# Moving one batch's k and q flips into the next pass, W1 loads ahead of k, q and v, and split work later in the first pass of a fused attention + MLP kernel

## The chip, the cores and the metric

One core of one Trainium2 chip. The metric is the device time of a run in microseconds (us). A change counts as faster or slower when it moves the time by over 2%. Differences under 1% matter here, so the experiments were timed in five rounds beside runs of the kernel before on the same chip (three rounds for two of them), and compared by ratio. All runs were in the fast state, with a granted TensorE clock of 0.991 to 1.0.

## The reference

```python
attn = softmax(q @ k.T / 8)                   # 8 batches, 16 q heads on 4 kv heads, 384 tokens, dim 64
x    = (attn @ v) as [8, 384, 1024]
u    = x + lam * (w_tok @ (alpha1 * x + beta1))     # token mixing, w_tok is 384 x 384
out  = u + lam * (relu((alpha2 * u + beta2) @ w_ch1) @ w_ch2)   # 1024 -> 4096 -> 1024
```

All inputs and the output are float32; the kernel multiplies in bfloat16. W1 is w_ch1 and W2 is w_ch2.

## The kernel before: the parts that matter

The kernel makes eight passes, one for each batch's MLP. A pass has a first half, h (16 chunks, each of which reads one W1 tile of 512 KB from a ring of five; the ReLU of its result is hT), and a second half, ch, which multiplies hT by W2 (W2 stays in SBUF). The attention of batch b+1 is woven into pass b. Its q and k must first be turned ("flipped") so that the head dimension lies on partitions. For batch 1 TensorE does this inside the first pass's h; from batch 2 on it is done by DMA transposes that SP issues. The last flips of a pass, those of a2 (alpha2 * u) into a2T, feed the next pass's h. In the first pass VectorE also does the "split", which writes the rows of alpha2 and lam as sums of bfloat16 parts, and a "spread" copies such rows to all partitions with matmuls. PE, the matmul engine TensorE, writes its sums into banks of PSUM; the kernel uses a bank again only when VectorE or ScalarE has read it.

```python
def flip_k(b):   # one DMA transpose of 12 blocks of 128 x 128
    nc.sync.dma_start_transpose(out=kT..., in_=k2s[b]...)
def flip_q(b, i=0, n=NP):   # two head pairs a call: 6 blocks; four calls for a batch
    nc.sync.dma_start_transpose(out=qT[:, i:i + n]..., in_=qrs[b]...)

def main(b):            # one pass; every yield lets woven work be emitted
    for c in range(NCH):                  # h: 16 chunks, two slots per h group
        ...  # 2 x 8 matmuls with the chunk's W1 tile; ReLU on ScalarE or VectorE
        if b or c + RING < NCH:
            load_w1(b * NCH + c + RING)   # refills the ring, from GpSimd's queue
        if b == 0 and c == NCH - 1:
            load_next(2)                  # k casts, q and v loads of batch 2
            for i in range(RING):
                load_w1(NCH + i)
    ...                                   # ch: 6 groups of 32 matmuls, eight slots each

# slots of ch in which pass b emits the flips for batch b + 2 (load_k, load_next: not for b == 0)
((1, load_k), (2, load_next), (34, flip_k), (36, flip_q, 0, 2), (37, flip_q, 2, 2),
 (42, flip_q, 4, 2), (43, flip_q, 6, 2))[2 * (b == 0):]
```

A slot fixes only where an instruction stands in the order of its engine. When it runs is decided by the engine and by its waits.

The softmax here doesn't subtract the row's maximum and nothing guards it: scores larger than these inputs give would overflow.

## Time and profile before

| | before |
|---|---|
| time, median (lowest to highest of 4) | 805.95 us (805.39 to 806.19) |
| PE busy, span of the profiled run | 788.9 us of 805.1 |
| first h matmul of passes 1, 2, 3, 4 | 30.89, 135.39, 234.06, 330.71 us |
| second to third pass; third to fourth | 98.67; 96.65 us |
| DMA row of the page | transfer engines at nine tenths or more of each slice until about 200 us |

The distance from one pass's first h matmul to the next one's is the most useful number of this case. From the third pass on it is 96.64 or 96.65 us in nearly every kernel below; what is over that in "second to third" is lost in the second pass. The prediction further down shows the lines of the profile that carry the argument.

### The profile page before, as it was taken

What the parts mean: (1) busy time and instruction counts of PE and PEld (TensorE: products, weight loads), DVE (VectorE), ACT (ScalarE), POOL (GpSimd) and SP (SyncE); (2) the same over time, 40 slices, a digit from 0 to 9 for tenths busy, and PEclk for the clock granted to TensorE, in tenths of its full rate; (3) what the DMA queues carried; (4) which work ended last, traced back from release to release, by engine and by line L of the source; (5) the groups of instructions that cost most, each with busy time, mean ns of one, the idle gap of its engine ahead of it and who ended that gap; (6) DMA issues with size and microseconds to landing.
All of it is one profiled execution on the core that took longest, in us unless ns stands there. A gap on an engine that the chain in (4) does not pass through costs nothing.

```text
span 805.1 us, 14151 instructions
## 1 busy us (share of the span) xinstructions
PE 788.9 (98%) x6056; PEld 452.3 (56%) x6123; DVE 342.6 (43%) x669; ACT 226.5 (28%) x309; POOL 179.4 (22%) x234
## 2 busy tenths in 40 slices
PE   7999999999999999999999999999999999999997
PEld 4766555655556555565555655556555655556545
DVE  7652465224552165422662236622366224552122
ACT  6623431223312334123321233222431224312100
POOL 7235430333003410135002340023400330003000
PEclk9999999999999999999999999999999999999999
DMA  9999999999269972899439991399915995139611
GB/s 186 196 207 198 203 203 182 184 198 144 54 129 184 198 112 57 151 190 197 72 78 164 195 199 50 86 176 195 166 44 117 162 198 91 48 61 181 89 40 40
DMA packets 234991, 113.17 MB, mean 141 GB/s; under 512 B 84392, under 2 KB 228784, under 8 KB 234928
## 3 DMA queue, kind: packets, MB, share of 16 engines
q0 software_dynamic: 170768, 83.47, 78.9%
q1 hardware_dynamic: 63616, 28.40, 14.5%
q8 instruction: 48, 0.79, 0.4%
q10 hardware_dynamic: 544, 0.39, 0.2%
q14 instruction: 15, 0.12, 0.0%
HBM read 170.53 MB, written 12.58 MB: 227 GB/s over the span
## 4 chain that ended last, share of the span: by engine, by line
PE 96%; DVE 1%; DMA 1%; issue 1%; POOL 0%; ACT 0%; POOLq 0%
PE ch L439 41%; PE h L406 40%; PE sc L214 4%; PE sc L249 4%; PE sc L270 4%; DMA stage<-in_moe_w_tok_dram 1%; PE h L165 1%; PE tok L270 1%; PE av L249 0%; PE ut L287 0%; DMA a2T<-a 0%; POOL v L110 0%; DVE hT L416 0%; DVE hT L525 0%; PE tp L200 0%
## 5 line engine op out<-in xcount | busy, mean ns | idle before, releaser
L439 PE MATMUL ch<-w,hT 128*128 128x512 bf16 (+2 forms) x1533 | 346.1, 370 | 4.4 <-issue 1.1
L406 PE MATMUL h<-a2T,w 128*128 128x384 bf16 (+1 forms) x2016 | 331.6, 326 | 2.5 <-DMA a2T<-a 1.5
L406 PEld LDWEIGHTS <-w 128*128 128x128 bf16 x2016 | 196.6, 98 | 133.1 <-issue 2.1
L133 POOL DMA_DIRECT2D w<-in_moe_w_ch_dram x128 | 112.0, 877 | 535.1 <-PE h L406 521.4
L439 PEld LDWEIGHTS <-hT 128*128 128x128 bf16 x1600 | 144.6, 98 | 152.6 <-issue 10.0
L223 ACT ACTIVATE es<-sc 128x1024 bf16<-128x1024 f32 x126 | 121.4, 1023 | 187.7 <-PE sc L214 178.8
L416 DVE TENSOR_SCALAR hT<-h,bias 128x384 bf16<-128x384 f32 x128 | 79.1, 618 | 219.0 <-PE h L406 218.5
L414 ACT ACTIVATE hT<-h,bias 128x384 bf16<-128x384 f32 x128 | 74.3, 581 | 304.8 <-PE h L406 304.2
L444 DVE TENSOR_TENSOR o<-ch,vecs 128x512 f32<-128x512 f32 (+2 forms) x50 | 33.4, 669 | 108.6 <-PE ch L439 108.6
L249 PEld LDWEIGHTS <-es 128*128 128x128 bf16 x1008 | 38.3, 97 | 13.2
L270 PEld LDWEIGHTS <-wtokT 128*128 128x128 bf16 x576 | 37.3, 98 | 13.6 <-DVE a L264 1.7
L214 PE MATMUL sc<-qT,kT 64*128 64x384 bf16 (+2 forms) x576 | 41.9, 271 | 1.2
L249 PE MATMUL sc<-v,es 128*128 128x65 bf16 x1008 | 39.8, 193 | 0.0
L254 DVE RECIPROCAL rinv<-sc 128x6 f32<-128x6 f32 x56 | 10.8, 193 | 67.4 <-PE sc L249 66.4
L277 DVE TENSOR_TENSOR x<-sc,x 128x384 f32<-128x384 f32 x56 | 31.0, 553 | 20.0 <-PE sc L270 20.0
L270 PE MATMUL sc<-a,wtokT 128*128 128x128 bf16 x504 | 37.3, 219 | 0.4
L214 PEld LDWEIGHTS <-kT 64*128 64x128 bf16 x576 | 21.7, 94 | 23.8 <-issue 18.4
L445 DVE TENSOR_TENSOR o<-o,x 128x512 f32<-128x512 f32 (+2 forms) x50 | 33.5, 670 | 1.7
L262 DVE TENSOR_TENSOR a1f<-x,vecs 128x384 f32<-128x384 f32 x56 | 31.6, 564 | 1.9
L264 DVE TENSOR_TENSOR a<-a1f,vecs 128x384 bf16<-128x384 f32 x56 | 31.4, 561 | 1.9
L281 DVE TENSOR_TENSOR a<-x,vecs 128x384 bf16<-128x384 f32 x56 | 31.3, 558 | 1.9
L255 DVE TENSOR_TENSOR x<-sc,rinv 128x384 f32<-128x384 f32 x56 | 31.2, 558 | 1.9
(75 smaller groups left out, 204.8 us busy)
## 6 DMA issues: line engine op xcount, KB each, us to landing
w<-in_moe_w_ch_dram POOLq DMA_DIRECT2D x136, 512.0 KB, 8.9
out_dram<-o SPq DMA_DIRECT2D x47, 256.0 KB, 2.0
q_raw<-in_q_dram POOLq DMA_DIRECT2D x28, 192.0 KB, 8.5
kst<-in_k_dram SPq DMA_DIRECT2D x16, 192.0 KB, 3.1
w<-in_moe_w_ch_dram POOLq DMA_DIRECT2D x1, 2048.0 KB, 16.5
w<-in_moe_w_ch_dram POOLq DMA_DIRECT2D x8, 256.0 KB, 10.0
v<-in_v_dram POOLq DMA_DIRECT2D x24, 64.0 KB, 8.6
a2T<-a SPq DMA_TRANSPOSE x56, 2.3
```

The lines of the kernel that those rows point to most:

```text
L133: nc.gpsimd.dma_start(out=t, in_=w1src[:, :, c * CW * P:(c + 1) * CW * P])
L214: nc.tensor.matmul(out=sc[:, hh, k % 4:k % 4 + n], lhsT=kT[r, sk, 2 * p // G, :], rhs=qT[r, p, st:st + n, :], start=True, stop=True)
L223: nc.scalar.activation(out=e, in_=sc, func=EXP, scale=scale_qk)
L249: nc.tensor.matmul(out=av[:, hh, sq, :], lhsT=ess[k // 4][:, m % 2, k % 4, :], rhs=vb[:, sk, hk, :], start=(sk == 0), stop=(sk == NST - 1))
L262: nc.vector.tensor_tensor(out=t, in0=x[:, :, cols(p)], in1=bc(g1, p), op=MUL)
L270: nc.tensor.matmul(out=ps[:, tt, :], lhsT=wtokT[:, st, tt * P:(tt + 1) * P], rhs=a1s[p][:, st, :], start=(st == 0), stop=(st == NST - 1 an ...
L406: nc.tensor.matmul(out=ps[:, :n], lhsT=w1[:, dt, j * P:(j + 1) * P], rhs=a2T[:, dt, :n], start=(dt == 0), stop=(dt == NDT - 1))
L414: nc.scalar.activation(out=hT[:, nt, :], in_=ps[:, :S], func=RELU, bias=c1)
L416: nc.vector.tensor_scalar(out=hT[:, nt, :], in0=ps[:, :S], scalar1=c1, scalar2=0.0, op0=ADD, op1=mybir.AluOpType.max)
L439: nc.tensor.matmul(out=ps[:, lo:hi], lhsT=hT[:, nt, ms * P:(ms + 1) * P], rhs=w2[:, nt, dw * 512 + lo:dw * 512 + hi], start=(nt == 0), sto ...
L444: nc.vector.tensor_tensor(out=o[:, lo:hi], in0=ps[:, lo:hi], in1=lam_t[:, c], op=MUL)
L445: nc.vector.tensor_tensor(out=o[:, lo:hi], in0=o[:, lo:hi], in1=x[:, ms, c], op=ADD)
```

## The change

Its intent: take the flips of batch 2 out of the busy end of the first pass, where they delay the a2T flips that the second pass waits for, and put them "late" in the second pass's h; load the W1 tiles first; spread the split of VectorE so that it does not hold a PSUM bank.

```diff
-                turns = {1: [(split, 2, 4)], 4: [(k_transpose, 0)], 8: [(q_transpose, 0, 2, "av")], 12: [(k_transpose, 2)]}
+                turns = {4: [(split, 2, 4, 0)], 8: [(split, 2, 4, 1)], 12: [(k_transpose, 0)],
+                         16: [(q_transpose, 0, 2, "av")], 20: [(k_transpose, 2)]}
...              # the other q transposes: 16 + 4 * i -> 24 + 4 * i; the spreads: 29 -> 34 and 45 -> 50
             if b == 0 and c == NCH - 1:
-                load_next(2)
                 for i in range(RING):
                     load_w1(NCH + i)
+                load_next(2)
...
+            moves = []
+            if b == 1:       # slots of h in the second pass
+                moves = [(0, 46 + 4 * i, flip_q, 2, 2 * i - 2, 2) if i else (0, 46, flip_k, 2) for i in range(5)]
+            if 0 < b < B - 2:      # later passes: as before
+                moves += [(1, 1, load_k, b + 2), (1, 2, load_next, b + 2), (1, 34, flip_k, b + 2), ...]
```

More of the change, by code (lines that the diff above doesn't have):

```diff
@@ L350, in side @@
             if b == 1:
-                turns = {1: [(split, 2, 4)], 4: [(k_transpose, 0)], 8: [(q_transpose, 0, 2, "av")], 12: [(k_transpose, 2)]}
+                turns = {4: [(split, 2, 4, 0)], 8: [(split, 2, 4, 1)], 12: [(k_transpose, 0)],
+                         16: [(q_transpose, 0, 2, "av")], 20: [(k_transpose, 2)]}
                 for i in range(3):
-                    turns[16 + 4 * i] = [(q_transpose, 2 + 2 * i, 2, "av")]
+                    turns[24 + 4 * i] = [(q_transpose, 2 + 2 * i, 2, "av")]
                 for i in range(4):
-                    turns[29 + 4 * i] = [(spread, (2 * i, 2 * i + 1), (1, 3), "tp", "ACT")]
+                    turns[34 + 4 * i] = [(spread, (2 * i, 2 * i + 1), (1, 3), "tp", "ACT")]
                 for i in range(2):
-                    turns[45 + 4 * i] = [(spread, range(4 * i, 4 * i + 4), (3, 4), "av", "ACT")]
+                    turns[50 + 4 * i] = [(spread, range(4 * i, 4 * i + 4), (3, 4), "av", "ACT")]
             return turns, {
@@ L555 @@
             us = side(b + 1) if b + 1 < B else ({}, {})
-            if b + 2 < B:
-                for u, f, *a in ((1, load_k), (2, load_next), (34, flip_k), (36, flip_q, 0, 2), (37, flip_q, 2, 2),
-                                 (42, flip_q, 4, 2), (43, flip_q, 6, 2))[2 * (b == 0):]:
-                    us[1].setdefault(u, []).append((f, b + 2, *a))
+            moves = []
+            if b == 1:
+                moves = [(0, 46 + 4 * i, flip_q, 2, 2 * i - 2, 2) if i else (0, 46, flip_k, 2) for i in range(5)]
+            if 0 < b < B - 2:
+                moves += [(1, 1, load_k, b + 2), (1, 2, load_next, b + 2), (1, 34, flip_k, b + 2), (1, 36, flip_q, b + 2, 0, 2),
+                          (1, 37, flip_q, b + 2, 2, 2), (1, 42, flip_q, b + 2, 4, 2), (1, 43, flip_q, b + 2, 6, 2)]
+            for i, u, *m in moves:
+                us[i].setdefault(u, []).append(m)
             done = [0, 0]
```

## The prediction

> **What bounds the kernel now.** I read the page first, for the busy shares and the slices; then the chain of waits around the ends of the passes; then the list of PE's waits; then the timelines of SP and PE where the chain left PE; last the DMA view of short windows. "Pass n" is the MLP of batch n (its first half is h, 16 chunks of one W1 tile each; its second half is ch); the attention of batch n+1 runs inside it.
>
> ```profile
> PE 788.9 (98%) x6056; PEld 452.3 (56%) x6123; DVE 342.6 (43%) x669; ACT 226.5 (28%) x309; POOL 179.4 (22%) x234
> DMA  9999999999269972899439991399915995139611
> PE 96%; DVE 1%; DMA 1%; issue 1%; POOL 0%; ACT 0%; POOLq 0%
> ```
>
> PE is the bound: 98% busy and 96% of the chain. The change takes no matmul away (the two built programs have the same 12194 rows on PE), so it can only win from the 16 us in which PE is not busy, and much of that lies in the start-up, which it does not touch. The DMA row is the other thing to see: ten nines at the left. The transfers are saturated for the first 200 us, and only later do they have holes.
>
> ```profile
> PE h L406 <- DMA a2T<-a: 1.5, 1, 1.5
> PE h L406 <- DVE hT L416: 0.8, 1, 0.8
> PEld L406 <- DMA w<-in_moe_w_ch_dram: 0.3, 1, 0.3
> ```
>
> These are the waits the change can reach. The first is at the start of the second pass, and the chain of waits shows it with its neighbours:
>
> ```profile
> 130.38 5.03 PE ch L439 x24
> 135.41 3.03 DMA a2T<-a
> 138.47 1.62 PE h L406 x9
> ```
>
> PE ran six of its h matmuls at 135.39, stopped at the seventh for one a2T piece and at the eighth for the last one, until 138.48. Nine matmuls ran in those 3.09 us at about 0.163 us each in the steady state, less the last one just begun: about 1.95 us are lost. The third pass started at 234.22 and the fourth at 330.87 (96.65 us apart), while second to third is 234.22 - 135.39 = 98.83: 2.2 us too long, which is the 1.95 and the 0.3 of the weight wait. Why the a2T pieces are late is in SP's timeline:
>
> ```profile
> 120.83 3.72 SPq L118 DMA_TRANSPOSE kT<-k  x1
> 126.24 1.57 SPq L292 DMA_TRANSPOSE a2T<-a  x1
> 127.91 5.38 SPq L122 DMA_TRANSPOSE qT<-q_raw  x2
> 133.38 0.53 SPq L446 DMA_DIRECT2D out_dram<-o  x1
> 134.00 2.62 SPq L292 DMA_TRANSPOSE a2T<-a  x2
> ```
>
> The last a2 was ready at 131.56 (VectorE's timeline), but SP was still issuing the two q flips, 5.38 us in place of 2.96 us for the same pair one pass later.
>
> **What the Trainium skill says.** "DMA: Bandwidth & Descriptors", section "Queues, rings and completion order": each engine serves its queue rows in turn, packet by packet. This trace agrees. Between 128 and 131 us, while W1 (q0) and a q flip (q1) ran together:
>
> ```profile
> q0 software_dynamic: 667, 0.34, 81.8%
> q1 hardware_dynamic: 660, 0.17, 42.7%
> ```
>
> Equal counts: in the 2.77 us that were active, about 240 packets/us each. W1 alone, 152 to 164 us:
>
> ```profile
> q0 software_dynamic: 4656, 2.34, 144.2%
> w<-in_moe_w_ch_dram POOLq DMA_DIRECT2D x5, 512.0 KB, 9.5
> ```
>
> That is 388 packets/us. Same page, "Anatomy of one DMA": the wait for a semaphore is made by the issuing sequencer, and the transfer engines just consume their queues; so an issue keeps its place behind what its own sequencer holds ahead of it, and SP's lines above show this. Same page, "Latency and other measured facts": 261 GB/s for a DMA transpose. Here the kT flip alone (0.39 MB, at 220.7 to 222.7) took 2.0 us, about 197 GB/s; I use the trace.
>
> **The change part by part.**
>
> (1) The split and the turns in the first pass. Before, five VectorE operations of the split stood together, 40.82 to 43.05 us, so that the bank of the fifth h group was freed late: the 0.84 wait at 45.01. From the start of the fifth group (39.41) to the eleventh (its ReLU at 51.11 less 1.31 less 0.33 of transposes: 49.45), six groups of 1.31 us and three turns of 0.33 need 8.84; it took 10.04, so 1.2 us are lost. After: only the cast and the multiply (0.59 + 0.47) stand ahead of that ReLU; VectorE would end it at about 43.65, and PE wants the bank at 43.33: 0.3 lost. The second half of the split falls behind it and costs nothing. But two of the three turns move later, so PE reaches the eleventh group at about 47.9, and its W1 tile lands at 48.40 in the trace (it stands behind the 2 MB W2 load and can't come earlier). So about 0.9 is lost in place of 1.2: a gain of 0.3, not 0.84. The spreads go to where ScalarE is free: 0.
>
> (2) Flips out of the first pass's ch. SP then has only the last out and the two a2T issues: ready at 130.5 and 131.56, landing 2.3 us after issue when the DMA is quiet. The flips' 4608 packets no longer share with W1 and q, so the queue, which before ran dry at about 133.5, should be dry at about 130. Landing at about 134, over 1 us before the pass starts: the 1.95 us go.
>
> (3) W1 ahead of k, q and v. The five tiles land at about 111 to 122 in place of 119 to 135. Pass 1 had not waited for them: 0 by itself.
>
> (4) The flips in the second pass. The new place is late in h in program order, but an order of issue is not a time. In the built program the flip of k stands on SP right behind the last out of pass 0, and waits only for the last score matmul of batch 1 and the cast on GpSimd, both long done. SP does nothing else in h. So all five flips go out at the start of the pass, not in its last third. Let T be its start. The last out's two VectorE steps end at T+1.6, the out is issued to T+2.2, k to T+3.6, each q takes 1.25 us, to T+8.6 at least; the loads of the next k follow. The first W1 of the pass (for chunk 5) is issued at T+2.7 and its packets flow from about T+4.8 (140.40 to 142.4 in the trace). By then k is nearly through (1536 packets at 780/us), and about 3500 flip packets remain. Shared at 240/us each they need 14.6 us, in which W1 loses 148 packets/us: 2160 packets, or 5.6 us. The k loads (512 packets) then cost about 1.2 us: about 7 us together, where the pass before lost 2.4 to its two late flips, k loads and ramp.
>
> What does W1 have to spare? A tile is 1024 packets, 2.64 us alone; a chunk is 2.60 us of PE: nothing to catch up with. Chunk 8's tile is the fourth: T+4.8 + 4096/388 (10.6) + 7.0 + about 1.75 from the packet count to the last landing (from the trace) = T+24.1; PE needs it at T+20.8. The same sum for before gives T'+19.5, and its landing at 157.22 is that, with T' = 137.7. So PE would wait about 3.3 us at chunks 7 to 8, and 0.04 per chunk after that: 3.6 us in the pass, less the 0.3 that it had.
>
> Sum: -0.3 - 1.95 + 3.3 = about +1.0 us on 806.0.
>
> **The rivals.**
>
> (A) The intended result: the flips are small beside 41.6 us and hidden, and the kernel gains about 2.3 to 2.5 us: 803.6. For it: five tiles are in SBUF at T, the first refill is needed only at T+13, and nothing else contends. Against it: the weight stream already has no spare rate, and the trace shows a one-to-one sharing with flips.
>
> (B) The last a2T pieces are late all the same, because W1 comes first, and q and v with their small packets are still landing at 131. Then the 1.95 stays in part and the time is about 807 to 809. Against it: without 4608 flip packets the queue ends earlier, and the third pass absorbs its own a2T with 0.7 us to spare though SP was issuing flips.
>
> (C) Contention worse than counted: the ramp loss before (about 2 us) adds to the sharing rather than hiding in it; PE waits 5 us, 808.5.
>
> **Range and chances.** My sum says 807.0; I take a wait of 3.6 +- 1.3 us, which gives 805.7 to 808.3, and give (A) about a quarter, which pulls the lower end to 803.6 and the middle a little down: 806.8, range 803.6 to 808.7. Two per cent would be 16 us, as much as all the idle time PE has, and no step here is near that in either direction: 0.01 faster, 0.98 same, 0.01 slower.
>
> **What would show it right or wrong.** (1) The wait for hT by VectorE near 45 us shrinks to under 0.4, and one for a W1 tile of about 0.5 appears near 48. (2) The wait for a2T at the second pass's start is gone. (4) SP issues kT and qT within 10 us of that start, not 30 us into it; in that stretch q1 and q0 show equal packet counts; and PE's list of waits shows W1 with 2 to 5 us in the second pass, first some 18 to 21 us after its start. If the flips sit late in h, or W1's landings stay under PE's needs, step (4) is wrong and (A) holds. All later passes must be 96.65 us apart as before; anything else would be a cause that I have not seen.

## The result, and the profile after

The changed kernel takes 810.41 us (810.09 to 811.25, 4 runs) against 805.95. The ratio is 1.0058, interval 1.0040 to 1.0075: slower, by about 4.5 us, though within 2%. (Ratios here and below are the mean time of one kernel's fast runs over that of the kernel before in the same rounds, so not quite the ratio of the medians quoted.) The prediction had the sign, but the time lies outside its range.

The waits of PE, kernel after:

```profile
PE h L407 <- DMA w<-in_moe_w_ch_dram: 5.8, 5, 2.2
```

The waits for a2T and for hT are gone from the list, and a wait for W1, hardly there before, is its longest (5.1 us of it in the second pass, the rest in the first). PE's timeline of the second pass, kernel after (start, duration, then what; in brackets how long PE was idle and for whom):

```profile
134.32 15.94 PE L407 MATMUL h<-a2T,w 128*128 128x384 bf16 x96
152.45 2.77 PE L407 MATMUL h<-a2T,w 128*128 128x384 bf16 x16 [2.19 <-DMA w<-in_moe_w_ch_dram]
156.65 2.77 PE L407 MATMUL h<-a2T,w 128*128 128x384 bf16 x16 [1.42 <-DMA w<-in_moe_w_ch_dram]
160.00 10.73 PE L407 MATMUL h<-a2T,w 128*128 128x384 bf16 x64 [0.58 <-DMA w<-in_moe_w_ch_dram]
171.66 10.59 PE L407 MATMUL h<-a2T,w 128*128 128x384 bf16 x63 [0.93 <-DMA w<-in_moe_w_ch_dram]
```

The pass starts without a stall at 134.32. PE then runs six chunks (96 matmuls) and stops at nearly every tile until chunk 8, and once more at chunk 12. The third pass starts at 237.30, so second to third is 102.98 us, 6.3 us over 96.65, where the kernel before had 2.0. SP's timeline shows when the flips went out, kernel after:

```profile
129.44 2.48 SPq L292 DMA_TRANSPOSE a2T<-a  x2
135.97 0.34 SPq L447 DMA_DIRECT2D out_dram<-o  x1
136.41 1.47 SPq L118 DMA_TRANSPOSE kT<-k  x1
137.97 9.67 SPq L122 DMA_TRANSPOSE qT<-q_raw  x4
147.70 1.10 SPq L95 DMA_DIRECT2D kst<-in_k_dram  x2
```

The two a2T issues now follow their data at once (131.92 at the latest, where it was 136.62). But the flips leave 2.1 us after the pass began, not 30 us into it, where their slot suggests. And SP needs 9.67 us to issue four q flips.

The transfer queues, kernel after, in three stretches (q0 carries W1, q1 what SP issues; packets, MB, share). First 139 to 148 us, then 148 to 155, then 158 to 166:

```profile
q0 software_dynamic: 1405, 0.71, 75.3%
q1 hardware_dynamic: 1963, 0.49, 54.4%
```

```profile
q0 software_dynamic: 1707, 0.86, 89.4%
q1 hardware_dynamic: 1704, 0.42, 47.6%
```

```profile
q0 software_dynamic: 3127, 1.58, 145.1%
q1 hardware_dynamic: 7, 0.00, 0.2%
```

The last stretch is W1 alone: 391 packets/us. The middle one is the sharing: 244 each. In the first, W1's first packet came at 139.76, so its 1405 are about 170 packets/us, less than the 244 of the middle stretch.

### The profile page after: what moved, and what is told of

Its sections match the earlier page's. It is cut to its first block, busy times and chain, and to the rows that moved or that the text cites. A ratio compares the mean times of both kernels' runs of the same rounds, so it can differ in the third digit from the quotient of the medians.

```text
span 808.3 us, 14151 instructions
## 1 busy us (share of the span) xinstructions
PE 789.8 (98%) x6056; PEld 451.7 (56%) x6123; DVE 342.1 (42%) x669; ACT 226.9 (28%) x309; POOL 179.5 (22%) x234
## 4 chain that ended last, share of the span: by engine, by line
PE 84%; DMA 9%; issue 4%; POOL 1%; DVE 1%; POOLq 0%
PE ch L440 37%; PE h L407 36%; DMA w<-in_moe_w_ch_dram 9%; PE sc L214 4%; PE sc L249 3%; PE sc L270 3%; POOL w L133 1%; POOL v L110 0%; DVE o L445 0%; POOL qg L498 0%; PE tp L200 0%; PE vec L327 0%; DVE o L446 0%; POOL w L138 0%; DVE a1f L262 0%
```

## The experiments

Twelve kernels were run, in three groups of four; each group shares the runs of the kernel before on its chip (medians 806.62, 806.21 and 806.65). "Second to third" is read from each profiled run. It is finer than the time, because the times of the kernel before alone spread over 4.4 to 6.5 us in those runs, but it is one execution for each kernel. The record marks the output of all twelve as correct, also of the three that are wrong on purpose, so that check does not tell whether a flip is missing; that is read from the code.

| run | ratio to before (interval) | second to third pass, us |
|---|---|---|
| before; after | 1; 1.0058 (1.0040 to 1.0075) | 98.67; 102.98 |
| flips_only | 1.0047 (1.0032 to 1.0061) | 102.64 |
| split_only | 1.0003 (0.9990 to 1.0015) | 101.61 |
| flips_back | 1.0007 (0.9995 to 1.0019) | 98.37 |
| no_flips (wrong result) | 0.9965 (0.9953 to 0.9978) | 96.65 |
| late_gate | 1.0032 (1.0021 to 1.0043) | 101.49 |
| gate_hold | 1.0141 (1.0116 to 1.0165) | 110.42 |
| plain_copies (wrong result) | 0.9984 (0.9974 to 0.9994) | 98.30 |
| q_after_a2t | 0.9985 (0.9970 to 1.0000) | 96.65 |
| q_after_split | 0.9973 (0.9962 to 0.9984) | 96.91 |
| flips_early | 0.9987 (0.9974 to 1.0000) | 98.24 |
| k_loads_later | 1.0022 (1.0012 to 1.0032) | 101.25 |
| two_q_flips (wrong result) | 1.0016 (1.0004 to 1.0028) | 100.75 |

### Which part costs: flips_only, split_only, flips_back, no_flips

flips_only takes the kernel before and replaces its list of flips by the changed kernel's `moves`, and nothing else.

> The kernel before with one part of the change: the third batch's five flips stand in the second pass's h; load order, split and turns as before. Theory (the flips, issued at the start of the pass, share the DMA engines with W1 and PE then waits for weights): five flips issued within 12 us of the start of the second pass, W1 waits of 5 to 6 us there, second to third pass about 103 us apart, time 4.2 us over before (810). Rival 1 (loading W1 ahead of k, q and v is what costs): no W1 wait over 0.5 us, the a2T wait gone, 804. Rival 2 (the moved split and turns cost): the same as rival 1 here, 804.

Measured: 810.88 us against 806.62, second to third 102.64 us, the flips issued from 137.52 to 148.96. The a2T wait is gone and W1 waits have come, though the list (kernel flips_only) has less of them than the 5 to 6 us expected:

```profile
PE h L406 <- DMA w<-in_moe_w_ch_dram: 3.5, 4, 2.2
```

This part alone makes nearly the whole difference, and both rivals fall.

split_only takes the kernel before with the changed kernel's `turns` alone.

> The kernel before with the split and the turns moved alone. Theory: the 0.8 us wait for hT by VectorE goes, a W1 wait of 0.6 to 0.7 us appears in its place near 47 us; gain 0.2 to 0.3 us in the first pass's h, which the late a2T of the second pass may swallow; time 805.6 to 806.0, not to be told from before. Rival 2: 2 us or more slower.

Measured: no difference in time (0.9990 to 1.0015). First to second pass was 103.98 us in place of 104.51, so the first pass gained; but the wait for a2T was 3.4 us in this execution, where before had 1.5, and took it back. The W1 wait was 0.3, not 0.6. Rival 2 is out: the interval ends at 1.2 us. The 101.61 us also shows how far a single execution can lie from the mean where PE waits for a2T.

flips_back takes the changed kernel with before's list of flips.

```diff
-            moves = []
-            if b == 1: ...            # and the lines that add them
+            if b + 2 < B:
+                for u, f, *a in (... (34, flip_k), (36, flip_q, 0, 2), (37, flip_q, 2, 2), (42, ...), (43, ...))[2 * (b == 0):]:
```

> The changed kernel with the five flips put back into the first pass's ch, the W1 loads still first and the split still moved. Theory: the W1 wait in the second pass falls from 5.1 to under 1 us; q lands only at about 127 to 130 us, so SP holds the last two a2T issues behind the q flips, and a wait for a2T of 0.3 to 2 us comes back; time 804 to 806. Rival 1 (load order): stays within 1 us of the changed kernel, 809.5 to 811.

Measured: the W1 wait is gone, an a2T wait of 1.4 us is back, the ratio is 1.0007. The time in microseconds (807.76) lies above what was expected, as does that of the kernel before on this chip; the ratio is what counts. The load order is not the cause, and gains nothing by itself while SP still holds a2T behind the q flips.

no_flips leaves the third batch's flips out.

```diff
-                moves = [(0, 46 + 4 * i, flip_q, 2, 2 * i - 2, 2) if i else (0, 46, flip_k, 2) for i in range(5)]
+                moves = []
```

> The changed kernel with the third batch's flips left out altogether (a wrong result on purpose: its scores use the second batch's k and q). Theory: with nothing but the next k loads beside W1, the W1 wait in the second pass is under 0.6 us and there is no a2T wait: the passes are 96.7 to 97 us apart and the time is 803.3 to 804.3. Rival (the k loads, or the ramp of the W1 stream itself, cause the wait): W1 waits of 2 us or more stay, 806 or more.

Measured: second to third 96.65 us, 804.28 us, and PE runs the second pass's h in one piece (kernel no_flips):

```profile
133.77 41.76 PE L407 MATMUL h<-a2T,w 128*128 128x384 bf16 x256
```

So the flips' presence in this stretch is the cause of the whole 6.3 us. Part of it goes by way of the k loads: without flips ahead of them SP issued these at 135.84, before the W1 stream, and not at 147.70. The ramp of the W1 stream by itself costs PE nothing.

### When should they go: late_gate, gate_hold, q_after_a2t, q_after_split, flips_early

late_gate makes SP wait for the ReLU of the 23rd hT row before the flips, as the change seems to have meant. Only the first flip is held so; the other four follow it at once, and not four slots apart.

```diff
+    def gate(nt):
+        g = sb.tile([P, 2], bf, tag="gate", name="gate", bufs=1)
+        nc.sync.dma_start(out=g, in_=hT[:, nt, :2])
...
+                moves = [(0, 46, gate, 22)]
-                moves = [(0, 46 + 4 * i, ...
+                moves += [(0, 46 + 4 * i, ...
```

> The changed kernel with a 4-byte-per-partition copy of the 23rd hT row ahead of the flips on the same issuing engine, so that they can only go out when the ReLU of that row is done, about 30 us into the second pass: the moment that the change's place in program order suggests. Theory: flips then start 30 us into the pass; only the last two or three W1 tiles of the pass (chunks 13 to 15) are hurried by PE, and each microsecond of sharing costs W1 148 packets, so PE waits 2 to 3 us for weights, at chunks 14 and 15; 3 to 4 us under the changed kernel (806.5 to 807.5). Rival A (the intended result): no wait, 804.

Measured: better than the changed kernel, but 1.0032 of before, more than I had expected. The W1 wait was only 0.7 us. What I had overlooked took its place. PE's waits of kernel late_gate:

```profile
PE sc L214 <- DMA qT<-q_raw: 2.5, 1, 2.5
PE h L411 <- DMA w<-in_moe_w_ch_dram: 0.7, 1, 0.7
```

The flips went out from 165.81 to 181.79, sharing mostly with W1 tiles of the third pass that are not urgent at all, and the first scores of batch 2 waited for them. The two waits are 3.2 of the 4.8 us lost; the list does not show the rest. So flips issued together at the moment that the change's slot suggests did not pay either.

gate_hold has the gate at the 29th row, and was meant to hold the next pass's W1 tiles back.

```diff
-            if b or c + RING < NCH:
+            if b > 1 or c + RING < NCH:
...
-            if b == 0 and c == NCH - 1:
+            if b < 2 and c == NCH - 1:
                 for i in range(RING):
-                    load_w1(NCH + i)
+                    load_w1((b + 1) * NCH + i)
+                moves = [(0, 58, gate, 28)]       # flips follow in slots 58 to 62
```

> The same gate on the 29th hT row (about 37.7 us into the pass), the flips one after another behind it, and the five W1 tiles of the third pass held back until the second pass's h is over. Theory: the last W1 tile that PE needs lands at about 38.4 us, so flips meet no W1; no wait for W1 or a2T, at most 1 us of waiting for kT or qT by the first scores; second to third pass 96.7 to 97.7 us apart; 2 to 2.5 us faster than before on the same chip (about 804.3) and 6 us faster than the changed kernel. If something other than the overlap of flips with W1 were the cause, it would stay above before.

Measured: 818.58 us, a plain miss. I made the change's own mistake: the loads stand later in the program, but GpSimd had nothing else to do and issued them when the ring's tiles came free, five times from 166.98 to 177.39. So they were in flight beside the flips, and the scores waited for the first flips (kernel gate_hold, SP and then PE):

```profile
174.50 3.02 SPq L118 DMA_TRANSPOSE kT<-k  x1
177.61 12.82 SPq L122 DMA_TRANSPOSE qT<-q_raw  x4
```

```profile
190.09 1.46 PE L214 MATMUL sc<-qT,kT 64*128 64x384 bf16 x12 [12.15 <-DMA qT<-q_raw]
```

Late flips fail twice: W1 for the next pass fills the queue, and the scores need the flips at once. A real hold was not tried.

q_after_a2t goes the other way: before, with all four q flips behind the last a2T flips. Two of the four stood there already; the other two move.

```diff
-                for u, f, *a in (... (36, flip_q, 0, 2), (37, flip_q, 2, 2), (42, flip_q, 4, 2), (43, flip_q, 6, 2))[2 * (b == 0):]:
+                late_q = [42, 43, 44, 45] if b == 0 else [36, 37, 42, 43]
+                for u, f, *a in (... *((u, flip_q, 2 * i, 2) for i, u in enumerate(late_q)))[2 * (b == 0):]:
```

> The kernel before with one thing changed: for the third batch the four q flips are issued behind the last two a2T flips, not ahead of them. Theory: the a2T wait of 1.5 to 2 us goes or falls under 0.7; the q flips run mostly before the second pass's W1 stream begins (4.8 us into it), so PE waits at most 1 us for weights; second to third pass 97 to 97.8 us apart; 1 to 2 us faster than before.

Measured: second to third 96.65 us, no a2T wait and no W1 wait. In time 0.9985, about 1.2 us, with an interval that reaches 1. q_after_split adds the moved split.

> The kernel before with the split and turns moved, and with the four q flips of the third batch issued behind the last two a2T flips. Theory: both gains add where no W1 tile is late: first to second pass about 103.5 us (1.0 less), second to third 96.7 us (2.0 less); 2 to 3 us faster than before, level with the kernel that had no flips at all (0.9965 of before), and with a right result.

Measured: first to second pass 103.50 us in place of 104.51, second to third 96.91; 0.9973, about 2.2 us faster than before, with all flips in place. This version beats both kernels, by less than the 2% that would count as faster. SP's and PE's lines of the same stretch, kernel q_after_split:

```profile
129.56 2.48 SPq L292 DMA_TRANSPOSE a2T<-a  x2
132.13 5.24 SPq L122 DMA_TRANSPOSE qT<-q_raw  x4
```

```profile
134.44 42.02 PE L407 MATMUL h<-a2T,w 128*128 128x384 bf16 x256
```

Four q flips are issued in 5.24 us, beside almost no W1, where the changed kernel needed 9.67.

flips_early is the changed kernel with all five flips one place earlier: ahead of the first pass's last out.

```diff
-            if b == 1:
-                moves = [(0, 46 + 4 * i, flip_q, 2, 2 * i - 2, 2) if i else (0, 46, flip_k, 2) for i in range(5)]
+            if b == 0:
+                moves = [(1, 42 + i, flip_q, 2, 2 * i - 2, 2) if i else (1, 42, flip_k, 2) for i in range(5)]
```

> The changed kernel with the same five flips, in the same order and behind the same W1-first loads, issued about 4 us earlier: ahead of the first pass's last out and not behind it. Theory: they start about 132 us, 2 us before the second pass, take 6 us alone and are through when the W1 stream begins 4.8 us into the pass; PE waits under 0.6 us for W1, second to third pass 96.7 to 97.3 us, 2 to 3 us faster than before and 6 to 7 faster than the changed kernel. Rival (flips near the start of the second pass cost whatever W1 does): 4 us or more of waiting stay.

Measured: second to third 98.24 us and a W1 wait of 1.0 us in the list. The flips were issued from 132.57 to 139.68 and the k loads up to 141.69, so both reached further into the W1 stream than I had said, and the gain over before was 0.13%, not 2 to 3 us. The main point holds: the same flips, about 4 us earlier, cost 1.6 us in place of 6.3.

### What the flips cost by: plain_copies, k_loads_later, two_q_flips

plain_copies moves the same bytes with ordinary DMAs.

```diff
     def flip_q(b, i=0, n=NP):
+        if b == 2:
+            nc.sync.dma_start(out=qT[:, i:i + n]..., in_=qrs[b]...)     # same bytes, no transpose; flip_k likewise
+            return
```

> The changed kernel with the third batch's five flips replaced by plain copies of the same bytes between the same tiles, in long rows (a wrong result on purpose). Theory (the engines share packet by packet, and flips are 4608 packets of 256 bytes): the same 1.18 MB in long packets is about 4.5 times the out stores' 0.26 MB, which cost W1 0.7 us apiece in the trace of before, so W1 loses about 3 us in place of 6 or more, and PE waits 0.5 to 2 us for weights in place of 5 to 6. Rival (bytes count, not packets): 5 us of waiting stay.

Measured: second to third 98.30 us, so 1.65 us lost in place of 6.3; faster than before (0.9984). The bytes are the same, but SP issued the copies in 3.2 us (137.46 to 140.63) where the flips took 11.2, so half of them, 0.59 of 1.18 MB, had gone before W1's first packet at 140.48; in the changed kernel 0.39 MB had. A cost by bytes would so have kept about three quarters (0.59 to 0.79 MB) of what the flips cost beside W1, and only 1.65 us are left, k loads included: the number of bytes is not what costs. That it is the number of packets (384 beside W1, for 3072) fits, but a flip differs from a copy in more than its packets and the k loads went out about 8 us earlier in the pass too, so this run does not separate these.

k_loads_later moves the next k loads and what depends on them into the second pass's ch.

```diff
-                moves += [(1, 1, load_k, b + 2), (1, 2, load_next, b + 2), ...
+                moves += [(1, 9 if b == 1 else 1, load_k, b + 2), (1, 12 if b == 1 else 2, load_next, b + 2), ...
```

> The changed kernel with the next k loads and what follows them (casts, q, v) issued later, in the second pass's ch, so that only the flips share with W1. Theory: the k loads took W1 about 590 packets at 155 to 158 us, 1.5 us; the wait for W1 falls by 1.2 to 1.7 us, second to third pass 101.2 to 101.8 us in place of 103.0, still 2.5 us or more slower than before. Rival: the k loads are the main cost: under 98.5 us.

Measured: 101.25 us, 1.7 less than the changed kernel; its third to fourth pass was 0.2 longer than usual. As the theory had it; the rival falls.

two_q_flips ends the list of flips after the k flip and two q flips (`range(3)` for `range(5)`).

> The changed kernel without the last two q flips (a wrong result on purpose): 1536 packets fewer of 4608. Theory: each packet that shares costs W1 its 1.64 ns, 2.5 us for these, and with less stalling perhaps 3.5: second to third pass 99.5 to 100.5 us in place of 103.0. Rival (a fixed cost of flips beside W1, such as stops of the engines at each flip or at the start): about 102 or more, or near 97 if only the late flips matter.

Measured: 100.75 us, 2.2 less, a little outside what was expected. The two missing flips are 1536 packets, so about 1.4 ns of PE time each; the k loads also went out 6 us earlier in the pass. Neither form of the rival (102 or more, or near 97) fits: with fewer flips the cost falls. That it is in proportion to them, one such run does not show.

## Why the prediction was wrong

**What bounds the kernel was read rightly.** One number of it was not: the prediction's "98.83" takes the start of the third pass from the chain (234.22), but its first h matmul ran at 234.06, so 98.67, and 2.0 us too long where it has 2.2.

**Step (1) was right in the profiled execution, partly by luck.** The wait for hT by VectorE is gone, and a W1 wait stands in its place (kernel after):

```profile
47.52 0.83 PE L407 MATMUL h<-a2T,w 128*128 128x385 bf16 x4 [0.66 <-DMA w<-in_moe_w_ch_dram]
```

From the end of the early h groups to ch the first pass took 40.75 us in place of 40.93: 0.2 gained where 0.3 was predicted. But that tile can come earlier than the prediction held. In seven of the eleven profiled kernels with the moved split (no_flips and q_after_split among them) it was not late, and the stretch took 39.92 us, 1.0 less than before.

**Step (2) was right.** The last a2T landed at 133.21, before the pass began, and the 1.95 us are gone. **Step (3) was right too:** the W1 tiles landed at 111.8 to 125.1 and no one had waited for them.

**Step (4) was right in its mechanism.** SP issued the flips at the start of the pass because nothing held them; W1 and flips shared packet for packet (1707 and 1704); PE waited for weights; the later passes are as before. **Its size was wrong,** and that is where the prediction failed: PE lost 6.3 us in the pass, and not 3.6. The sum for the tile of chunk 8 was 4.8 + 10.6 + 7.0 + 1.75, a landing 24.1 us after the pass's start T. It landed at 159.96, which is T + 25.6. Counting q0's packets in the trace, against 388/us, from 139.6, just before W1's first packet:

| stretch | W1 moved | at 388/us | lost |
|---|---|---|---|
| 139.6 to 148 | 1405 | 3259 | 1854 = 4.8 us |
| 148 to 155 (sharing) | 1707 | 2716 | 1009 = 2.6 us |
| 155 to 158 (k loads) | 581 | 1164 | 583 = 1.5 us |

That is 8.9 us, but not all of it is due to flips and k loads. In no_flips, with almost nothing else in flight, W1's own first 8.4 us (138.5 to 146.9) moved

```profile
q0 software_dynamic: 2525, 1.28, 124.0%
```

which is 734 packets, or 1.9 us, short of 388/us. So the flips took about 5.5 us and the k loads 1.5, together the 7 that were predicted. (late_gate's start was only 1.1 us short, by which the flips' part would be 6.3; two starts alone differ by that much.) **The term that was missing is W1's own slow start:** the sum let it run at 388 packets/us from its first packet. The landings say the same. In no_flips chunk 8's tile landed at 153.01, T + 19.2, where the sum without its 7.0 gives T + 17.15: 2.1 us later (1.6 in late_gate). Alone this costs PE nothing, since PE wants the tile at T + 20.8; on top of the sharing PE pays for it. This is rival (C), to which I gave too little room: the loss of the ramp adds to the sharing, and does not hide in it. Its own number, 5 us and 808.5, was still too small.

PE began chunk 8 at 160.00, 4.9 us late where 3.3 was predicted. Its first wait came at chunk 6, and not at 7 to 8. The rest is mostly chunk 12: from chunk 8 to there 11.66 us passed in place of 10.4, where I had counted 0.04 us per chunk. The tile there landed 3.7 us after the one before it, in place of 2.6; the kernel before had the same gap at the same tile (3.4 us), but still a little stock to absorb most of it. One more size was off: the issue of the flips ended at T + 13.3, where the sum had T + 8.6 as the least.

The experiments agree, if the terms simply add: of the 6.3 us, 1.7 go with the k loads, 2.2 with the last two q flips, and 2.4 are left for the first two (the k flip's packets had all gone before W1's first). In the sum: 0.2 gained in the first pass, 4.3 lost between the second and the third, which is 4.1; the profiled execution started 0.9 us faster in code that did not change, so its span is only 3.2 us longer (808.3 against 805.1).

**What stays open.** Why W1 starts slowly when it is alone: 2525 packets in the 8.4 us of no_flips, 2815 in those of late_gate, for 3259 at the full rate. Beside the flips there is also one stop, at 142.7 to 143.4, in which hardly a packet of either queue went; the kernel before has such a stop at 127.3 to 128.2, also while flips and W1 were in flight. Both came about 1 us after a fetch of 16 KB of instructions had started, and counting packets in all fourteen traces ties the two together. Between 90 and 200 us, 25 such fetches began with flips and GpSimd's loads both moving (50 packets or more of each in the next microsecond); within 2.1 us of every one of them came 0.4 us with at most 14 packets of the two. After the 57 fetches beside 200 packets or more of such loads and no flips, no 0.4 us had fewer than 74. No run moved a fetch, so this is a count and not an experiment, and its reason is open.

## What to carry to other kernels

The slot in which an instruction is emitted is an order, not a time. An issue runs as soon as its own engine reaches it and its waits have passed, so ask what stands ahead of it on that engine and what it waits for; if it must be late, something must hold it. Where a stream of weights runs at the transfer limit with no rate to spare (2.64 us a tile for 2.60 us of work), all that shared the engines with it was paid for by the consumer, packet for packet, and the stream's own slow start, harmless alone, was paid for on top. Put such transfers into the gap before the stream begins: the four q flips began 3.7 us after, 0.8 us before and 2.3 us before the start of the pass in after, flips_early and q_after_a2t, and the pass lost 6.3 us, 1.6 us and nothing (in the last one the k flip went earlier still).

## What the Trainium skill lacked or had wrong

- "DMA: Bandwidth & Descriptors", section "Queues, rings and completion order", says that an engine serves its queues in turn by packets. The runs agree, but the page gives no rate for a transpose beside a load, and that is what decided here: 388 to 391 W1 packets/us alone, 244 beside 243 flip packets/us (kernel after, 148 to 155 us), and only about 170 from W1's first packet to 148 us, part of which is W1's own slow start.
- The same page, section "Latency and other measured facts", has 261 GB/s for a DMA transpose whose middle dimension is not contiguous, and 350 to 400 for a contiguous one (the prediction left the condition out). One kT flip alone moved 0.39 MB in 2.0 us here, about 197 GB/s; q flips that followed one another moved 252 GB/s (q_after_split, 134.4 to 136.8 us). So the first figure is not wrong, but a single flip of this size does not reach it.
- I found it on no page that the issue of a transpose itself takes longer while loads are in flight: SP needed 5.24 us for four q flips beside almost no W1 (q_after_split), and 9.67 to 12.8 us beside W1 (after, gate_hold).
- Nor is there anything on the stops of both queues described above (0.7 us at 142.7 in the kernel after, and after each of 25 instruction fetches that met flips and loads together, in fourteen traces); their cause is open.
